# Tile starts at multiples of 256 bytes, and the low parts of the last stage's input chunks computed on GpSimd

## The chip, the cores and the metric

The kernel runs on one core of a Trainium2 chip. TensorE (PE in the profile; its weight loads are PEld), VectorE (DVE), ScalarE (ACT) and GpSimd (POOL) compute; SyncE (SP) issues the DMAs. The engines run side by side and wait for each other through semaphores. The metric is the device time of one execution in microseconds.

## The reference

For `x` of 2048 rows and 640 columns, the kernel computes `g * a + (1 - g) * b`, all in float32:

```python
g = sigmoid((x * gate_w).sum(-1, keepdims=True))
q, k, v = split(x @ wqkv, 32 heads of 20)
phi(p) = concat(softmax(p @ w_phi), softmax(-(p @ w_phi)))      # 40 features a head
kv, z = phi(k)^T v, phi(k).sum over the rows
a = ((phi(q) @ kv) / (phi(q) @ z + 1e-6)) @ wo
b = silu(x @ w1) @ w2                                            # 1728 hidden columns
```

`a` is linear attention: the keys and values of all rows are first summed into a small table per head (`kv`), then each row's query features are multiplied with it. `b` is a feed-forward block.

## The kernel before

To reach float32 accuracy on TensorE, every operand of a large product is held as a high part (the value rounded to TensorE's one-pass format) and a low part (the remainder). A product then takes three passes: high times high, high times low, low times high. The helper `split` (lines 120 to 123) makes the two parts: ScalarE copies the high part, and VectorE or GpSimd subtracts it from the source for the low part. Its two lines, 121 and 123, therefore carry the splits of all stages; tile names tell them apart.

The work runs in three stages, each ordered by hand (`inorder` fixes the order of instructions per engine; the DMA issues on SP are left to the framework's scheduler):

1. **Keys and values** (about 0 to 200 us of the span). The weights `wh`/`wl` (high and low part, two tiles of tag `big`) are formed, then 16 row tiles are projected (line 473, 500 and 282 columns at a time) and summed into `kv` (lines 443 and 454).
2. **Feed-forward** (about 200 to 560 us). For each of four blocks of 512 rows and each of 14 hidden tiles, `ph` (line 521) multiplies a tile of `w1` with `x`, and `acc` (line 709) multiplies a tile of `w2` with the activated hidden tile `u`. Each product streams 512 columns past a 128 by 128 weight tile; both have 15 matmuls for a hidden tile, 10 for the rest tile `w_r`.
3. **Queries and output** (about 560 to the end). Rows go in chunks of 256. A step (`step(u)`) transposes the features of chunk u (`pT`, line 990), projects two row tiles with the fused query weights (`pq`, line 432, 320 columns), multiplies features with `kv` (`pn`, line 1123), copies the numerators to `oT` (lines 1136 to 1146) and multiplies them with `wo` (`pa`, line 1165, 256 columns, 80 matmuls a chunk). VectorE takes maxima, differences and sums of the query features (lines 416 to 423, 794, 810); GpSimd multiplies the features with the normalizer and its inverse (lines 807 and 843) and adds the feed-forward part to the output (line 1183).

The input of stage 3, apart from the first chunks, comes through `raw` tiles: a chunk is three DMAs (`xb_load`, two of 512 columns' width and one of 256), and each is split by `xb_split` into an `xb` tile. `x_next(k)` splits the next k of them and issues the load of the one four further on into the `raw` tile that this frees (`x_ahead`). The line `xb_split(p, "dve")` puts the low part on VectorE. `step` calls `x_next(2)` at its start and `x_next(1)` in its middle. The first chunk's three splits are outside `x_next` and have the low part on GpSimd.

All tiles lie in pools that follow one another in SBUF. Each tile is rounded up to 32 bytes, so a tile's start follows from the sizes of all that stand before it:

| tiles | what they hold | start modulo 256, before |
|---|---|---|
| tag `big`, first | `wh`; later `f` tiles of hidden tiles 7, 8 and 9 (`w1`), 7 and 8 (`w2`); later `wo` | 128 |
| tag `big`, second | `wl`; later `f` tiles of hidden tiles 5, 6 (`w1`), 4, 5, 6 (`w2`); later `wq` | 0 |
| tag `raw`, four | inputs on arrival | 128, 160, 192, 224 |
| tags `x`, `w`, `u` | input chunks, weights of hidden tiles 0 to 4 (`w1`), 0 to 3 (`w2`), activations | 0 |
| pools `ta`, then `fp`, then `tb` | `ta`: features and values of stage 1; `fp`: `w1` of hidden tiles 10 to 12, `w2` of 9 to 12, `w_r`; `tb`: `oT`, the rest rows of `wo` (`wor_s`), `ez`, `y` | 224 |

In the feed-forward stage every weight slice (128 columns, 512 bytes) lies a multiple of 512 bytes behind its tile's start, so it has that tile's remainder.

Of the kernel before, what the change touches and what calls it, by code (L numbers as in the profile page):

```python
# [8 lines left out]
F32 = mybir.dt.float32  # L9
# [7 lines left out]
P = 128  # L17
S = 2048
D = 640
# [3 lines left out]
NC = D // P  # L23
# [7 lines left out]
GW = GR * DH  # L31
# [4 lines left out]
RC = 2 * REST  # L36
# [15 lines left out]
EB = 2  # L52
KXB = 1
WC = 2 * D + 2
WS = WC + 2
BIG = 2 * NC * D + 32
CUTS = (0, 500, 1000, WC)
RW = 114
NEARLY = 3
# [4 lines left out]
def mix_kernel(ctx: ExitStack, tc: tile.TileContext, xT, wqT, wkc, wkr, wv, bd, bdc, cst, wo, w1, w1r, w2, out):  # L64
    nc = tc.nc

    cp = ctx.enter_context(tc.tile_pool(name="cp", bufs=1))
    wp = ctx.enter_context(tc.tile_pool(name="wp", bufs=1))
# [3 lines left out]
    def opened(name, **kw):  # L72
        open_pools[name] = tc.tile_pool(name=name, bufs=1, **kw)
        return open_pools[name].__enter__()
# [6 lines left out]
    fu = opened("fu")  # L81
    ta = opened("ta")
# [16 lines left out]
        return ps.tile([P, 512], F32, tag=f"single{k % 4}", name=name, bufs=1)  # L99

    def raw(name):
        return wp.tile([P, D + 2], F32, tag="raw", name=name, bufs=4)

    def slot(name, pool=None, tag="x", bufs=7):
        return (pool or wp).tile([P, 2, 512], F32R, tag=tag, name=name, bufs=bufs)

    def big_tile(name):
        return wp.tile([P, BIG], F32R, tag="big", name=name, bufs=2)

    def big(name):  # L110
        return big_tile(name)[:, : 2 * NC * D].rearrange("p (c s d) -> p c s d", c=NC, s=2)
# [5 lines left out]
    def wslot(name, dt=F32):  # L117
        return fq.tile([P, 2 * D], dt, tag="w", name=name, bufs=NPRE)

    def split(hi, lo, src, lo_eng="dve"):  # L120
        nc.scalar.copy(hi, src)  # L121
        eng = nc.vector if lo_eng == "dve" else nc.gpsimd
        eng.tensor_tensor(lo, src, hi.bitcast(F32), op=ALU.subtract)  # L123
# [4 lines left out]
    @contextmanager  # L128
    def inorder(*engines):

        traced = nc.cur_bb.bb.instructions
        n = len(traced)
        yield
        prev = {}
        for i in traced[n:]:
            if i.engine in engines:
                if i.engine in prev:
                    tc.add_manual_dep(
                        i,
                        prev[i.engine],  # L140
                        mybir.DependencyInfo(mybir.DependencyClass.NoSync, mybir.DependencyReason.DATA),
                        reason="inorder",
                    )
                prev[i.engine] = i.name
# [6 lines left out]
    stk = cp.tile([P, 4], F32, name="stk")  # L151
    warms = cp.tile([P, 1], F32, name="warms")
    ones = cp.tile([P, P], F32R, name="ones")
    stage = [ta.tile([P, 2, 2 * D], F32, tag="ph", name=f"stage{k}", bufs=2) for k in range(2)]
    stf = [t.rearrange("p a d -> p (a d)") for t in stage]
    st0 = [t[:, k * D : (k + 1) * D] for t in stf for k in range(3)][:NC]
# [59 lines left out]
    def xb_split(p, lo_eng="pool"):  # L216
        u, c = XP[p]
        r = xb.pop(p)
        t = slot(f"xb_{u}_{c}")
        split(t[:, 0, : r.shape[1]], t[:, 1, : r.shape[1]], r, lo_eng)  # L220
        if c == 0:
            X["t", u] = []
        X["t", u].extend(t[:, :, k * 256 : (k + 1) * 256] for k in range(r.shape[1] // 256))
# [3 lines left out]
    def load_fused(gi):  # L227
        n = min(GW, D - gi * GW)
        rq[gi] = r = raw(f"wTq{gi}")[:, :D]
        nc.sync.dma_start(r[:n, :], wqT[gi * GW : gi * GW + n, :])  # L230
# [64 lines left out]
    def flat(name):  # L295
        return ta.tile([P, D + 2], F32, tag="kx", name=name, bufs=KXB)
# [45 lines left out]
    kvp1 = [None] + [ps.tile([P, 512], F32, name=f"kvq{k}") for k in (1, 2)]  # L342

    def v_weights(c):
        r = ta.tile([P, 2 * D], F32, tag="e", name="wvr1", bufs=EB)[:, : D + 2] if c == 1 else flat(f"wvr{c}") if c == 2 else raw(f"wvr{c}")
        nc.sync.dma_start(r, wv[c * P : (c + 1) * P, :])
        split(WKV[0][:, c, D:WC], WKV[1][:, c, D:WC], r)

# [367 lines left out]
    r = raw("w1rr")  # L716
# [4 lines left out]
    r = raw("w2rr")  # L721
# [9 lines left out]
    def wo_load(c):  # L731
        wor_raw[c] = r = raw(f"wo{c}")
        nc.sync.dma_start(r[:, :D], wo[c * P : (c + 1) * P, :])
# [146 lines left out]
    def kvl_load(k):  # L880
        kvb[k] = r = raw(f"kvl{k}")[:KD, :D]
        nc.sync.dma_start(r, kv_d[KD:KF, k * D : (k + 1) * D])

    def kvl_sum(k):

        r = kvb.pop(k)
        a = kvb["kvm"][:, k * D : (k + 1) * D]
        nc.vector.tensor_tensor(a, a, r, op=ALU.add)
# [53 lines left out]
    def load_gates(b):  # L942
        if b == 0:
            pg = bank("pg")
            nc.tensor.transpose(pg[:NT, :P], g1, ident)
            gT = fp.tile([NT, P], F32, name="gT")
            nc.scalar.copy(gT, pg[:NT, :P])
            nc.sync.dma_start(g_d, gT)
        gates[b] = fp.tile([P, 512], F32, tag="G1", name=f"G1_{b}", bufs=1)
        nc.sync.dma_start(gates[b], g_d.rearrange("t p -> (t p)")[b * 512 : (b + 1) * 512].partition_broadcast(P))  # L950
# [17 lines left out]
    def last_dense(n, *extra):  # L968

        part = h_parts(NB - 1, order[n])  # L970
        us[order[n]] = next(part)
        for w in extra:
            next(w)
        next(part)
        if 1 < n < NF:
            add(n - 2)
        for w in extra:
            next(w)
# [33 lines left out]
    with inorder(PE, DVE, ACT, POOL):  # L1012
        last_dense(2)
        last_dense(3)
        load_gates(NB - 1)
        load_fused(0)
        last_dense(4)
        WQ = big("wq")
        zbc = wslot("zbc")
        nc.sync.dma_start(zbc, kv_d[KF].partition_broadcast(P))  # L1020

        def fuse(gi):
            return fused(kvb["bd"], WQ[:, :, 0, :], WQ[:, :, 1, :], gi)

        load_fused(1)
        kvl_load(0)
        last_dense(5, fuse(0))
        kvl_sum(0)
        load_fused(2)
        kvl_load(1)  # L1030
        last_dense(6, fuse(1))
        kvl_sum(1)
        WO = big("wo")
        load_fused(3)
        wo_load(0)
        last_dense(7, fuse(2))
        wo_split(0)
        load_fused(4)
        wo_load(1)
        wo_load(2)  # L1040
        last_dense(8, fuse(3))
        wo_split(1)
        wo_split(2)
        load_fused(5)
        wo_load(3)
        wo_load(4)
        kvw = wslot("kvw")[:GW, : 2 * NG * CT].rearrange("p (j f) -> p j f", f=CT)
        kvwr = fu.tile([RC, GW], F32, name="kvwr")
        w = make_kvw()
        last_dense(9, w)  # L1050
        w = fuse(4)
        next(w)
        next(w)
        wo_split(3)
        wo_split(4)
        for p in range(3):
            xb_load(p)
        last_dense(10, fuse(5))
        t = 2 * NP - 4
        q_tile(t)  # L1060
        last_dense(11)
        q_rest(t)
        xb_split(0)
        t += 1
        q_tile(t)
        last_dense(12)
        q_rest(t)
        xb_split(1)
        t += 1
        q_tile(t)  # L1070
        last_dense(13)
        q_scale(t)
        t += 1
        q_open(t, q_proj(t))
        xb_split(2)
        acc_mm(0)
        q_feat(t)
        q_norm_sum(t - 1)
        q_parts(t - 1)
        acc_out(0)  # L1080
        q_inv(t - 1)
        q_weights(t - 1)
        q_mul(t - 1)
        q_norm(t)
        acc_mm(1)
        acc_out(1)
        acc_mm(2)
        acc_out(2)
        for i in range(4):
            t_mm(0, i, bank)  # L1090
            t_out(0, i)
        acc_mm(3)
        acc_out(3)
        q_sum(t)
        q_scale(t)
        acc_mm(4)
        acc_out(4)
        q_norm_sum(t)
        q_parts(t)
        q_inv(t)  # L1100
        q_weights(t)
        q_mul(t)
# [91 lines left out]

    def x_next(k):
        for p in range(xb_done[0], min(xb_done[0] + k, len(XP))):
            xb_split(p, "dve")
            x_ahead(p + 4)
            xb_done[0] = p + 1

# [21 lines left out]

    def step(u):
        a, b, c = 2 * u - 2, 2 * u - 1, 2 * u
        x_next(2)
        t_all(u, 0, 4)
        on(b, q_mm)
        on(a, q_norm_sum)
        t_all(u, 4, 6)
        spikes(b)  # L1230
        on(a, q_small)
        on(b, q_norm)
        on(a, q_mul)
        w_mm(u - 1, 0, 2)
        w_copy(u - 1, 0)
        w_add(u - 1, 0)
        on(b, q_sum)
        x_next(1)
        n_all(u)
        n_lo(u, 0)  # L1240
        on(b, q_norm_sum, q_small, q_mul)
        on(c, q_mm)
        w_mm(u - 1, 2, 2)
        spikes(c)
        w_copy(u - 1, 2)
        n_lo(u, 1)
        n_lo(u, 2)
        w_mm(u - 1, 4, 1)
        on(c, q_sum, q_norm)
        w_copy(u - 1, 4)  # L1250
        w_add(u - 1, 2)
        w_add(u - 1, 4)
# [109 lines left out]
```

## Time and profile before

| | |
|---|---|
| median of 3 runs | 756.83 us (756.64 to 757.03) |
| the profiled execution | 756.51 us, span 754.7 us from first to last instruction |
| TensorE busy | 748.6 us, 99% of the span, 4177 matmuls |
| VectorE, ScalarE, GpSimd busy | 370.0, 264.0, 243.9 us |
| granted TensorE clock | 1.00 throughout |

Views that are used below: the page's summary; the groups of instructions by line and tile (busy time, mean duration, idle time before them and who ended it); the chain of work that ended last, which gives start, length and number of instructions of each piece, so that length over number is the spacing from one matmul's start to the next; and the timeline, in which the columns are start, length, engine, line, operation and, in brackets, idle time of the engine and who ended it. A matmul's own duration (some 390 ns) overlaps with the next one's and isn't its price; the spacing is.

### The profile page before, as it was taken

How to read it: one execution, taken by the hardware profiler on the slowest of the kernel's cores; microseconds unless marked ns; L12 is line 12 of the kernel's file. 1: busy time of each engine (PE TensorE's matmuls, PEld its weight loads, DVE VectorE, ACT ScalarE, POOL GpSimd, SP SyncE). 2: the span in 40 equal slices, each digit the busy share in tenths (PEclk: the TensorE clock that was granted, in tenths of full speed). 3: DMA queues.
4: the chain of work that ended last, by engine and by line, in shares of the span. 5: the costliest groups of instructions: out<-in, count | busy, mean ns of one | idle time of the engine just before them, and what ended most of it. 6: DMA issues, size and time to landing. Idle time of an engine off the chain costs nothing.

```text
span 754.7 us, 10442 instructions
## 1 busy us (share of the span) xinstructions
PE 748.6 (99%) x4177; PEld 646.7 (86%) x4177; DVE 370.0 (49%) x634; ACT 264.0 (35%) x477; POOL 243.9 (32%) x143
## 2 busy tenths in 40 slices
PE   9999999999999999999999999999999999999998
PEld 7888888888888888888888888888898899999988
DVE  5676666676641221012210122123566898888752
ACT  5444444336542311113111121123453534345230
POOL 2488777768000000000000000000274367565540
PEclk9999999999999999999999999999999999999999
DMA  7111111113660120001200014122103132221222
GB/s 260 50 54 53 53 53 53 59 44 90 198 185 1 56 98 1 1 0 56 101 0 1 1 41 120 37 74 72 38 29 107 55 98 64 91 76 58 71 85 78
DMA packets 35304, 50.27 MB, mean 67 GB/s; under 512 B 3546, under 2 KB 22890, under 8 KB 35255
## 3 DMA queue, kind: packets, MB, share of 16 engines
q1 hardware_dynamic: 35255, 49.60, 20.9%
q8 instruction: 33, 0.54, 0.3%
q14 instruction: 16, 0.13, 0.1%
HBM read 38.48 MB, written 11.11 MB: 66 GB/s over the span
## 4 chain that ended last, share of the span: by engine, by line
PE 96%; DVE 2%; DMA 1%; issue 0%; ACT 0%; SPq 0%; DVEq 0%
PE acc L709 25%; PE ph L521 23%; PE kvp L473 16%; PE pa L1165 10%; PE pq L432 9%; PE pn L1123 3%; PE kv L443 2%; PE pT L990 2%; PE kvp L538 2%; PE kvp L331 1%; PE kvq L331 1%; PE pwq L234 1%; PE pwk L320 1%; DVE xb L123 1%; DMA wvr<-wv 1%
## 5 line engine op out<-in xcount | busy, mean ns | idle before, releaser
L123 DVE TENSOR_TENSOR u<-ph,u 128x512 fp32r<-128x512 f32 x48 | 33.2, 692 | 187.3 <-ACT u L121 187.3
L709 PE MATMUL acc<-u,w 128*128 128x512 f32 x480 | 115.2, 393 | 0.0
L709 PEld LDWEIGHTS acc<-u,w 128*128 128x128 f32 x480 | 89.6, 188 | 20.2
L892 POOL MEMSET kvw<- 120x40 f32 x1 | 0.1, 132 | 314.1 <-PE ph L521 314.1
L521 PE MATMUL ph<-xf,w 128*128 128x512 f32 x420 | 100.6, 392 | 0.0
L524 ACT ACTIVATE ph<-ph 128x512 f32<-128x512 f32 x48 | 27.9, 582 | 192.1 <-PE ph L521 192.0
L521 PEld LDWEIGHTS ph<-xf,w 128*128 128x128 f32 x420 | 78.7, 188 | 17.5
L473 PE MATMUL kvp<-wh,xa 128*128 128x500 f32 (+1 forms) x420 | 93.0, 357 | 0.0
L473 PEld LDWEIGHTS kvp<-wh,xa 128*128 128x128 f32 x420 | 71.4, 189 | 10.0
L1165 PE MATMUL pa<-oT,wo 128*128 128x256 f32 x600 | 77.8, 283 | 0.0
L807 POOL TENSOR_TENSOR ez<-eq,zbc 128x1280 f32<-128x1280 f32 x16 | 47.0, 2935 | 92.7 <-ACT eq L790 55.1
L1165 PEld LDWEIGHTS pa<-oT,wo 128*128 128x128 f32 x600 | 74.6, 189 | 0.8 <-DVE oT L1144 0.8
L709 PE MATMUL acc<-u,f 128*128 128x512 f32 x300 | 72.3, 392 | 0.0
L521 PE MATMUL ph<-xf,f 128*128 128x512 f32 x300 | 72.3, 392 | 0.0
L521 PEld LDWEIGHTS ph<-xf,f 128*128 128x128 f32 x300 | 56.4, 188 | 12.5
L709 PEld LDWEIGHTS acc<-u,f 128*128 128x128 f32 x300 | 56.2, 188 | 12.2
L432 PE MATMUL pq<-wq,xb 128*128 128x320 f32 x360 | 56.3, 313 | 1.0 <-DVE xb L123 0.8
L123 POOL TENSOR_TENSOR ph<-ek,ph 128x1280 fp32r<-128x1280 f32 x16 | 47.5, 2969 | 27.4 <-ACT ph L121 27.4
L432 PEld LDWEIGHTS pq<-wq,xb 128*128 128x128 f32 x360 | 52.9, 188 | 3.5 <-issue 1.6
L473 PE MATMUL kvp<-wl,xa 128*128 128x500 f32 (+1 forms) x210 | 47.6, 357 | 0.0
L790 ACT ACTIVATE eq<-eq 128x1280 f32<-128x1280 f32 x16 | 20.4, 1275 | 67.9 <-DVE eq L423 67.9
L501 POOL TENSOR_TENSOR ek<-ek,st 128x1280 f32<-128x1280 f32 x16 | 37.9, 2369 | 9.1 <-issue 6.1
(159 smaller groups left out, 1070.0 us busy)
## 6 DMA issues: line engine op xcount, KB each, us to landing
wr<-w SPq DMA_DIRECT2D x26, 320.0 KB, 3.9
xrf<-xT SPq DMA_DIRECT2D x20, 256.0 KB, 3.7
fb_d<-o SPq DMA_DIRECT2D x20, 256.0 KB, 2.4
y<-fb_d SPq DMA_DIRECT2D x16, 256.0 KB, 3.0
out<-y SPq DMA_DIRECT2D x16, 256.0 KB, 2.1
xra<-xT SPq DMA_DIRECT2D x14, 256.0 KB, 3.0
xrb<-xT SPq DMA_DIRECT2D x12, 256.0 KB, 2.6
wvr<-wv SPq DMA_DIRECT2D x5, 321.0 KB, 5.2
```

The costliest lines, as they stand in the source:

```text
L123: eng.tensor_tensor(lo, src, hi.bitcast(F32), op=ALU.subtract)
L331: nc.tensor.matmul(kv_cols(t, lo, hi), x_of(t)[c][:, hx, :], WKV[hw][:, c, lo:hi], start=(opens and hx == 0 and hw == 0), stop=(c == NC - ...
L432: nc.tensor.matmul(dst, xt[c][:, hx, :], w[:, c, hw, lo : lo + n], start=first, stop=(hx == 1 and c == NC - 1))
L473: nc.tensor.matmul(kv_cols(t, lo, hi), xt[c][:, hx, :], WKV[hw][:, c, lo:hi], start=(n == 0), stop=(n == 3 * NC - 1), skip_group_check=True,)
L501: nc.gpsimd.tensor_tensor(groups(e), groups(e), spread(st[:, 1, :]), op=ALU.mult)
L521: nc.tensor.matmul(ph, lhs, rhs, start=(n == 0), stop=(n == len(todo) - 1))
L524: nc.scalar.activation(hs, ph, AF.Silu)
L709: nc.tensor.matmul(acc[m], lhs, rhs, start=(f == order[0] and n == 0), stop=(f == order[-1] and n == len(todo) - 1))
L790: nc.scalar.activation(Q[t]["e"], Q[t]["e"], AF.Exp)
L807: nc.gpsimd.tensor_tensor(ez, Q[t]["e"], zbc, op=ALU.mult)
L1123: nc.tensor.matmul(pns[u, gp][side * CT : side * CT + lhs.shape[-1], a, :], lhs, f[:w, k * 256 : (k + 1) * 256], start=True, stop=True,)
L1165: nc.tensor.matmul(pa[:, a, :], WO[:, c, hw, ds] if c < NG else WOR[:, ds], o[:, ho, c, :] if c < NG else o[:GW, ho, c, :], start=(k == 0) ...
```

## The change

Four sizes change, one unused tile of 128 bytes is added, and the splits in `x_next` change their engine and place:

```diff
-BIG = 2 * NC * D + 32
+RAW = D + 16
+BIG = 2 * NC * D + 64
...
     def raw(name):
-        return wp.tile([P, D + 2], F32, tag="raw", name=name, bufs=4)
+        return wp.tile([P, RAW], F32, tag="raw", name=name, bufs=4)
...
     ones = cp.tile([P, P], F32R, name="ones")
+    cp.tile([P, 32], F32, name="pad")
...
-        r = ... else raw(f"wvr{c}")
+        r = ... else raw(f"wvr{c}")[:, : D + 2]
...
-        kvwr = fu.tile([RC, GW], F32, name="kvwr")
+        kvwr = fu.tile([RC, P], F32, name="kvwr")[:, :GW]
...
     def x_next(k):
         for p in range(xb_done[0], min(xb_done[0] + k, len(XP))):
-            xb_split(p, "dve")
+            xb_split(p)
...
     def step(u):
         a, b, c = 2 * u - 2, 2 * u - 1, 2 * u
-        x_next(2)
+        x_next(3)
...
         on(b, q_sum)
-        x_next(1)
         n_all(u)
```

Counted through: the constants' pool begins at byte 16,512 and had 1,280 bytes, so the first `big` tile began at 17,792 (69 times 256, and 128); with the pad it begins at 17,920 (70 times 256). A `big` tile grows from 25,728 to 25,856 bytes (101 times 256). The four `raw` tiles grow from 2,592 to 2,624 bytes each, 10,496 together (41 times 256); one by one they begin at remainders 0, 64, 128 and 192. `kvwr` grows from 480 to 512 bytes. The pools `ta`, `fp` and `tb` then begin at 175,360 (685 times 256) in place of 174,816 (682 times 256, and 224). So the `f` tiles, `wo`, the weights in `fp`, `oT` and `wor_s` all begin at multiples of 256 bytes. The rows of `wh` and `wl` are 5,136 bytes apart before and after, so their slices still begin at many remainders.

`xb_split(p)` without an engine puts the low part on GpSimd, in that engine's order at the place of the call: three low parts at the start of each of the steps 1 to 5 (15 instructions), ahead of the step's other work on GpSimd. The high parts stay on ScalarE; the third of each step moves from the middle to the start of ScalarE's order. The third load of a step is issued right after the two others.

More of the change, by code (lines that the diff above doesn't have):

```diff
@@ L344, in v_weights @@
     def v_weights(c):
-        r = ta.tile([P, 2 * D], F32, tag="e", name="wvr1", bufs=EB)[:, : D + 2] if c == 1 else flat(f"wvr{c}") if c == 2 else raw(f"wvr{c}")
+        r = ta.tile([P, 2 * D], F32, tag="e", name="wvr1", bufs=EB)[:, : D + 2] if c == 1 else flat(f"wvr{c}") if c == 2 else raw(f"wvr{c}")[:, : D + 2]
         nc.sync.dma_start(r, wv[c * P : (c + 1) * P, :])
```

## The prediction, made before the result was known

> **What bounds the kernel now.** First the page's head and its chain: TensorE is busy 99% of the span and carries 96% of the chain that ended last. Only two things can make this kernel faster: matmuls that follow each other more closely, or fewer waits of TensorE.
>
> ```profile
> span 754.7 us, 10442 instructions
> PE 748.6 (99%) x4177; PEld 646.7 (86%) x4177; DVE 370.0 (49%) x634; ACT 264.0 (35%) x477; POOL 243.9 (32%) x143
> ...
> PE 96%; DVE 2%; DMA 1%; issue 0%; ACT 0%; SPq 0%; DVEq 0%
> ```
>
> Next the chain of waits inside the feed-forward stage (second block of rows). Columns: start, length, piece, number of matmuls; nothing waits between the pieces.
>
> ```profile
> 299.65 3.40 PE acc L709 x15
> 303.05 3.40 PE ph L521 x15
> 306.45 3.41 PE acc L709 x15
> 309.86 3.49 PE ph L521 x15
> ...
> 325.98 3.48 PE acc L709 x15
> 329.46 3.49 PE ph L521 x15
> 332.95 3.49 PE acc L709 x15
> 336.44 3.50 PE ph L521 x15
> ...
> 345.77 3.50 PE acc L709 x15
> ```
>
> These are matmuls of one shape, yet they come at different spacings. By the order of the hidden tiles and the table of starts, the first three (`w2` of tile 3, `w1` of 6, `w2` of 4) have weights at remainder 0: 10.21 / 45 = 226.9 ns. 309.86 (`w1` of 7), 329.46 (`w1` of 9) and 325.98, 332.95 (`w2` of 7 and 8) have remainder 128: 13.95 / 60 = 232.5 ns. 336.44 (`w1` of 10) and 345.77 (`w2` of 9) have 224: 233.3 ns. Low addresses are slow (first `big` tile), middle ones fast, the highest slow again, so it is the remainder that fits, not the place.
>
> The last stage I read by the timeline, a steady step (from 647) beside the first one (from 598); each from the first `pn` over 24 `pn`, 30 `pq` and 48 `pa` matmuls to the next transposes.
>
> ```profile
> 598.28 2.38 PE L1123 MATMUL pn<-fT,kvw 120*64 120x256 f32 x20
> ...
> 601.33 2.49 PE L432 MATMUL pq<-wq,xb 128*128 128x320 f32 x14 [0.23 <-DVE sm L837]
> 604.62 2.61 PE L432 MATMUL pq<-wq,xb 128*128 128x320 f32 x16 [0.80 <-DVE xb L123]
> ...
> 612.81 1.37 PE L990 MATMUL pT<-ident,eq 128*120 128x128 f32 x11
> ```
>
> ```profile
> 647.23 2.38 PE L1123 MATMUL pn<-fT,kvw 120*64 120x256 f32 x20
> ...
> 660.21 1.91 PE L990 MATMUL pT<-ident,eq 128*120 128x128 f32 x16
> ```
>
> The same work takes 12.98 us in a steady step and 14.53 us in the first, so the two waits cost 1.55 us with the restarts behind them. The bracket names the low part `xb` on VectorE as one cause and a small VectorE instruction queued behind another `xb` as the other.
>
> **The change part by part.**
>
> *512-column matmuls.* The groups give the numbers.
>
> ```profile
> L709 PE MATMUL acc<-u,w 128*128 128x512 f32 x480 | 115.2, 393 | 0.0
> L521 PE MATMUL ph<-xf,w 128*128 128x512 f32 x420 | 100.6, 392 | 0.0
> ...
> L709 PE MATMUL acc<-u,f 128*128 128x512 f32 x300 | 72.3, 392 | 0.0
> L521 PE MATMUL ph<-xf,f 128*128 128x512 f32 x300 | 72.3, 392 | 0.0
> ...
> L709 PE MATMUL acc<-u,w_r 128*128 128x512 f32 x40 | 10.0, 395 | 0.0
> ```
>
> Of the 300 `ph<-xf,f`, three of five tiles lie in the first `big` tile (180 matmuls); of the 300 `acc<-u,f`, two of five (120): 300 at remainder 128. Of the 420 `ph<-xf,w`, 180 lie in `fp` (3 tiles, 15 matmuls, 4 blocks); of the 480 `acc<-u,w`, 240; with 40 of `w_r` in `acc` and 40 in `ph`, 500 at remainder 224. All come to 226.9 ns. The gain is 300 x 5.6 = 1.7 us and 500 x 6.4 = 3.2 us, 4.9 together. Ends: 0, if the start isn't the cause, and 800 x 6.4 = 5.1. Nothing covers or eats this gain: in these rows TensorE follows itself.
>
> A rule speaks against it. The Trainium skill, page "TensorE: Matmul & The Clock Gate", section "Step-by-step: what each phase is for", says that weights come through a read port of their own, so that loading the next ones takes no read bandwidth from the running matmul. By that alone a weight tile's start shouldn't change the spacing, and this term would be 0. The rows above differ by weights alone, so here the trace doesn't agree with it.
>
> *256-column matmuls of the output.* Both operands (`oT` at 224, `wo` at 128) become aligned, and no aligned row of that shape exists. The nearest rows by shape, from the chain in the key stage and in the last one:
>
> ```profile
> 102.17 6.82 PE kvp L473 x30
> ...
> 109.33 1.95 PE kvp L473 x15
> ```
>
> ```profile
> 614.73 4.40 PE pq L432 x30
> ...
> 654.64 5.73 PE pa L1165 x48
> ```
>
> Unaligned: 282 columns 130.0 ns, 500 columns 227.3, 512 columns about 233, and `pa` itself, 256 columns, 119.4. These lie near one line, about 0.445 ns a column and 5 ns. Aligned: `pq`, 320 columns, 146.7 ns, and 512 columns, 226.9: 0.418 ns a column and 13.0 ns. The lines cross near 280 columns; at 256 the aligned one gives 120.0 ns. So I take 640 x (120.0 - 119.4) = 0.4 us lost. The gaining end is a saving as large as that of a 512-column matmul, 6 ns: 640 x 6.0 = 3.8 us. I take the line, since it meets two aligned shapes and the other meets four unaligned ones.
>
> *Keys and values.* `wh` moves by 128 bytes, but its rows are 5,136 bytes apart, so slices keep beginning at all sorts of remainders, as they do in both halves now (227.3 and 130.0 above). I take 0. The ends are 0.5 us either way, about 1 ns on 420 + 70 matmuls.
>
> *The first loads.* Input and weight rows land at other remainders, and TensorE waits once for what they feed:
>
> ```profile
> 8.82 0.56 PE L331 MATMUL kvp<-wh,xa 128*128 128x360 f32 x2 [0.41 <-ACT wh L121]
> ```
>
> Bounds are a gain or a loss of that wait, 0.4 us; I take 0, since the transfer also reads memory, whose rows don't change. The Trainium skill, page "DMA: Bandwidth & Descriptors", section "How a descriptor splits into AXI transactions", has an unaligned transfer start with a partly unused 256-byte piece: a row of 2,568 bytes from remainder 224 would be 88 beats in place of 81, an estimate from that page. By it the wait would vanish.
>
> *Low parts to GpSimd.* Prices by the groups and the tile's own list:
>
> ```profile
> L123 DVE TENSOR_TENSOR xb<-xrb,xb 128x512 fp32r<-128x512 f32 x10 | 14.9, 1523 | 2.8 <-ACT xb L121 2.8
> ...
> L123 DVE TENSOR_TENSOR xb<-xrb,xb 128x256 fp32r<-128x256 f32 x5 | 9.2, 1849 | 0.0
> ```
>
> ```profile
> L123 POOL TENSOR_TENSOR xb<-xrb,xb x3: 733/1290/1294, 549.5 to 567.0; 128x512 fp32r<-128x512 f32 x2, 128x256 fp32r<-128x256 f32 x1
> ```
>
> VectorE loses 14.9 + 9.2 = 24.1 us, 4.8 a step; GpSimd gets 2 x 1.29 + 0.73 = 3.3 us a step. GpSimd's own steps, and what it does in one step:
>
> ```profile
> 591.54 2.94 POOL L807 TENSOR_TENSOR ez<-eq,zbc 128x1280 f32<-128x1280 f32 x1 [5.40 <-ACT eq L790]
> ...
> 652.66 1.30 POOL L1183 TENSOR_TENSOR y<-pac,y 128x512 f32<-128x512 f32 x1
> 654.07 2.37 POOL L843 TENSOR_TENSOR eq<-eq,sm 128x1280 f32<-128x1280 f32 x1
> 659.08 2.93 POOL L807 TENSOR_TENSOR ez<-eq,zbc 128x1280 f32<-128x1280 f32 x1 [2.64 <-ACT eq L790]
> 661.96 2.90 POOL L1183 TENSOR_TENSOR y<-pac,y 128x512 f32<-128x512 f32 x2
> 670.95 2.91 POOL L807 TENSOR_TENSOR ez<-eq,zbc 128x1280 f32<-128x1280 f32 x1 [6.09 <-DVE sm L837]
> ```
>
> ```profile
> 636.68:660.37 23.69, 23.69 (x189) 22.43 (x187) 20.80 (x30) 10.05 (x18) 14.84 (x8) 1.00 0.26 84
> ```
>
> The three pieces stand between 664.86 and 670.95, where GpSimd idles 6.09 us: they end at about 668.2, 2.8 us ahead of the next product, at no cost. Without that cover they would delay the feature product (654.07 to 656.44), which the transposes at 660.21 need: 3.8 us more of slack. In step 1 GpSimd ends its `ez` at 594.5 and the pieces at 597.8, before `pq` reads them (from 601). VectorE, rid of two `xb` there, waits for that `ez` instead and comes about 1 us sooner to line 837, for which TensorE waited 0.23 us. Both waits go: 1.55 us gained. Ends: 0 (VectorE still late) and 1.55.
>
> ScalarE's third copy comes ahead of the copies of the transposes; it delays these by 0.4 us, and TensorE reuses their banks only after 4.4 us of `pq`. SP: the three loads now wait for GpSimd's pieces; behind them in SP's queue may stand the output stores and the loads of `y`. These can come some 3.5 us later, and the addition that needs `y` (652.66 in the steady step, so 676.3 in the next) is after two more GpSimd products. I take 0; its price if it fails is rival D.
>
> *Sum*, against the profiled execution (756.51 us): - 4.9 + 0.4 - 1.55 = - 6.05, that is 750.5 us. The median shown is 0.3 us higher than that execution.
>
> **The rivals.**
> A: the 256-column matmuls gain like the 512-column ones. For it: same engine, both operands moved. Against: the two lines. 750.5 - 0.4 - 3.8 = 746.3 us.
> B: the start isn't the cause, and the alignment does nothing: only the 1.55 us remain, 755.0 us. Against it stand all nine feed-forward rows. (The skill's rule on weight loads, above, would have it so.)
> C: the alignment gains, but the first step's waits stay, because another VectorE or ScalarE instruction is as late: 752.0 us.
> D, the slower side: GpSimd's pieces, and behind them the loads and stores on SP, make the feature product late in every step. It takes a delay beyond the 3.8 us of slack; for a loss over all, TensorE must lose over 6.05 + 1.5 us in five steps, 1.5 a step, so a delay over 5.3 us. If pieces of 3.3 us behaved as three times as long (6.6 more, 2.8 beyond the slack), five steps would lose 14 us: 756.5 - 4.5 + 14 = 766 us. Against: by the window above (busy time of PE, PEld, DVE, ACT and POOL) GpSimd is 14.84 of 23.69 us busy in a step.
>
> **How the numbers follow.** Main case 0.55, A 0.27, C 0.08, B 0.06, D 0.04. About 0.2%, 1.5 us, is what can be told from no change. Main, A and C are faster; B lies just at that bound, and I count two thirds of it as same. Range 745.8 to 752.3: from A to C with half a microsecond for the first loads and the key stage; it leaves out B and D. The main case alone: 749.6 to 751.4.
>
> **What would show it.** All feed-forward pieces of 15 at 3.40 us; one that keeps 3.49 or 3.50 falsifies the first term. `pa` pieces of 48 at 5.76 us (main) or 5.45 (A). The first step's 14.53 us become 12.98, with no bracket naming `xb`, and steady steps stay at 23.7 us. Wrong would be a TensorE wait on GpSimd at the transposes (D), or a new wait of `pq` on ScalarE's copies (C).

## The result, and the profile after

The changed kernel takes 749.68 us (749.52 to 750.11) against 756.77 us: ratio 0.9907, 95% interval 0.989 to 0.9924. The forecast was 750.5 us, in a range of 745.8 to 752.3. The profiled execution took 749.73 us with a span of 748.0 us, 6.8 us less than the one before; the sum had said 6.05.

In the changed file most lines stand two further down (`ph` is line 523, `acc` 711, `pq` 434, `pa` 1167), the low part of `split` one further, at 124. The page's head and chain after:

```profile
span 748.0 us, 10444 instructions
PE 742.9 (99%) x4177; PEld 647.2 (87%) x4177; DVE 347.6 (46%) x619; ACT 263.8 (35%) x477; POOL 255.2 (34%) x158
...
PE 98%; DMA 1%; SPq 0%; ACT 0%; DVE 0%; issue 0%
```

TensorE has the same 4177 matmuls and is as full as before; VectorE, 2% of the chain before, has all but left it. The chain inside the same block of the feed-forward stage, with the same hidden tiles as in the prediction:

```profile
301.36 3.40 PE ph L523 x15
304.76 3.40 PE acc L711 x15
308.16 3.40 PE ph L523 x15
...
324.02 3.40 PE acc L711 x15
327.43 3.40 PE ph L523 x15
330.82 3.40 PE acc L711 x15
334.23 3.40 PE ph L523 x15
...
343.29 3.40 PE acc L711 x15
```

Every piece of 15 is at 3.40 us: the spacing is now 226.7 ns whichever pool holds the weights. The pieces that were at 3.48 to 3.50 are those from 308.16 on, except the `acc` pieces of tiles 5 and 6. In the key stage the chain shows a small shift that the prediction had left at 0: matmuls of 500 columns follow each other a little closer, those of 282 columns a little further apart:

```profile
102.14 6.77 PE kvp L475 x30
...
109.24 1.97 PE kvp L475 x15
```

The first step of the last stage, by TensorE's timeline:

```profile
592.85 2.38 PE L1125 MATMUL pn<-fT,kvw 120*64 120x256 f32 x20
...
595.59 4.66 PE L434 MATMUL pq<-wq,xb 128*128 128x320 f32 x30
...
605.85 1.91 PE L992 MATMUL pT<-ident,eq 128*120 128x128 f32 x16
```

`pq` is one piece of 30 without a bracket. From the first `pn` to the transposes it is 13.00 us, where it was 14.53. Of the last stage's pieces, those of 48 output matmuls got longer by the chain, 5.76 us in place of 5.73; those of 32 stayed at 3.82:

```profile
600.25 5.76 PE pa L1167 x48
```

Added over the spacings from one matmul's start to the next: the 800 feed-forward matmuls with formerly unaligned weights gave 4.8 us and the aligned ones beside them 0.3; `pq` and `pn` gave 1.6; the key stage 0.5; `pa` took 0.2, and the first 25 us took 0.1.

### The profile page after: what moved, and what is told of

Same layout as the page of the kernel before. It is cut to its first block, busy times and chain, and to the rows that moved or that the text cites. A ratio compares the mean times of both kernels' runs of the same rounds, so it can differ in the third digit from the quotient of the medians.

```text
span 748.0 us, 10444 instructions
## 1 busy us (share of the span) xinstructions
PE 742.9 (99%) x4177; PEld 647.2 (87%) x4177; DVE 347.6 (46%) x619; ACT 263.8 (35%) x477; POOL 255.2 (34%) x158
## 4 chain that ended last, share of the span: by engine, by line
PE 98%; DMA 1%; SPq 0%; ACT 0%; DVE 0%; issue 0%
PE acc L711 25%; PE ph L523 23%; PE kvp L475 16%; PE pa L1167 10%; PE pq L434 10%; PE pn L1125 3%; PE pT L992 2%; PE kv L445 2%; PE kvp L540 2%; PE kvp L333 1%; PE kvq L333 1%; PE pwq L236 1%; PE pwk L322 1%; DMA wvr<-wv 1%; PE kvp L456 0%; SPq L187 0%
## 5 line engine op out<-in xcount | busy, mean ns | idle before, releaser
L711 PE MATMUL acc<-u,w 128*128 128x512 f32 x480 | 113.6, 390 | 0.0
```

Of the source, the lines that this page charges most:

```text
L711: nc.tensor.matmul(acc[m], lhs, rhs, start=(f == order[0] and n == 0), stop=(f == order[-1] and n == len(todo) - 1))
```

## The experiments

The two theories to be told apart: the gain consists of two independent parts, operand starts (about 4.5 us) and the low parts' move (1.55 us); or one of them does all. Then, for the starts: an unaligned start lengthens the time per column, so that 512-column matmuls lose and 256-column ones do not (two lines); or it costs a fixed amount per matmul; or only weights count.

**The sizes alone** (`align_only`):

```diff
-            xb_split(p)
+            xb_split(p, "dve")
...
-        x_next(3)
+        x_next(2)
...
+        x_next(1)
         n_all(u)
```

> The changed kernel's sizes, but the low parts of the xb tiles on VectorE and at their old two places. Theory (two separate gains): feed-forward pieces of 15 matmuls at 3.40 us, output pieces of 48 at 5.76 us, and in the first step the stretch from pn to the next transposes back at 14.5 us with waits on the xb low part; about 1.55 us slower than the changed kernel, 751.2 us. Rival (the new starts of the raw tiles are what made the low parts come in time): VectorE's xb of 512 columns falls clearly below 1523 ns, the first step stays near 13.0 us, and the time is that of the changed kernel, 749.7 us.

Measured: 751.16 us (750.78 to 751.53), ratio 0.9926 (0.9912 to 0.994). TensorE's timeline in the first step has its two waits back:

```profile
592.63 2.38 PE L1125 MATMUL pn<-fT,kvw 120*64 120x256 f32 x20
...
595.69 2.49 PE L434 MATMUL pq<-wq,xb 128*128 128x320 f32 x14 [0.25 <-DVE sm L839]
598.98 2.61 PE L434 MATMUL pq<-wq,xb 128*128 128x320 f32 x16 [0.80 <-DVE xb L124]
...
607.19 1.04 PE L992 MATMUL pT<-ident,eq 128*120 128x128 f32 x8
```

That is 14.56 us, and the group of `xb` stays at 1518 ns. So the starts of the `raw` tiles have nothing to do with it.

**The move alone** (`move_only`):

```diff
-            xb_split(p, "dve")
+            xb_split(p)
...
-        x_next(2)
+        x_next(3)
...
-        x_next(1)
```

> The old sizes, with the low parts of the xb tiles on GpSimd at the start of each step. Theory: the first step falls from 14.53 to about 13.0 us, nothing else moves; 756.8 - 1.55 = 755.2 us. Rival (the waits go only because TensorE's spacing changed): the first step stays above 14 us and the time at 756.8 us.

Measured: 755.34 us (754.83 to 755.77), ratio 0.998 (0.9971 to 0.9989). The first step's stretch runs from 598.23 to 611.21, 12.98 us. The two parts add up: 756.83 - 751.16 = 5.7 and 756.83 - 755.34 = 1.5, together 7.2, against 7.1 for the whole change.

**The engine without the place** (`engine_only`): the changed kernel with the third split back in the middle of the step.

```diff
-        x_next(3)
+        x_next(2)
...
+        x_next(1)
         n_all(u)
```

> The changed kernel, but the third split of a step stays in the middle of the step; its low part then stands in GpSimd's order behind the addition to the output. Theory (the place is as necessary as the engine): that addition ends some 4.0 us after pq begins (653.96 against 649.97 in the steady step of the kernel before), the low part 0.7 us later, and pq reads it after about 2.0 us, so TensorE waits about 2.7 us in each of five steps: about 13 us slower than the changed kernel, 763 us. Rival (the engine alone matters): no wait, 749.7 us.

Measured: 770.0 us in a single execution, 20 us slower than the changed kernel and 13 slower than the kernel before. From 590 us on, by the view of waits, TensorE waits for nothing but the low part, five times, 12.9 us in all, of which 4.2 us in the first step and 2.2 in each of the others:

```profile
PE pq L434 <- POOL xb L124: 12.9, 5, 4.2
```

The chain of one step, in order of time:

```profile
639.96 4.42 PE pq L434 x30
...
644.40 0.82 DVE mmq L418
...
651.67 2.38 POOL eq L845
654.05 0.69 POOL y L1185
...
655.22 0.74 POOL xb L124
655.96 0.04 issue
656.00 4.15 PE pq L434 x16
...
667.65 4.42 PE pq L434 x30
```

The mechanism of the wait is the expected one, and so is its size, since 13 us were expected. The chain shows why the low part is late again in each step: the late `pq` makes the maxima late, these the exponentials and GpSimd's products, and behind those stands the next low part for which `pq` waits.

What wasn't expected is the rest of the loss. The 16 `pq` matmuls behind the wait take 4.15 us above, but 2.61 us one step earlier, behind a wait of the same length:

```profile
629.85 2.61 PE L434 MATMUL pq<-wq,xb 128*128 128x320 f32 x16 [2.17 <-POOL xb L124]
```

The granted TensorE clock is 0.59 from 656.00 to 660.15 us and 1.00 from 629.80 to 632.50. Over four of the five pieces behind a wait it is 0.59 to 0.62, and these take 3.93 to 4.15 us, about 5.8 us more together than at the full clock. So a step with the lower clock takes 27.7 us (639.96 to 667.65), 4.0 us more than the steady 23.7, and the step ahead of it 26.15 us (613.81 to 639.96), 2.4 us more. Waits and clock are 18.7 of the 20 us; the rest isn't assigned, and why the clock fell behind four of the waits and not behind the fifth stays open.

**The place without the engine** (`place_only`): three splits at the start, low parts on VectorE.

```diff
-            xb_split(p)
+            xb_split(p, "dve")
```

> The changed kernel with all three splits at the start of a step, but their low parts on VectorE. Theory (VectorE's load early in the step is what counts): VectorE spends 4.8 us at the start of a step in place of 2.9, so the wait for line 837's successor in the first step grows from 0.2 to about 2 us while the wait for the third low part goes; the first step's stretch comes to about 15.3 us, the steady steps stay at 23.7 us, and the time is about 752.0 us. Rival (only the late third split mattered): the first step at about 13.3 us, 750.0 us.

Measured: 750.28 us in a single execution, nearer to the rival. The stretch is 13.61 us, with one wait left:

```profile
592.79 2.38 PE L1125 MATMUL pn<-fT,kvw 120*64 120x256 f32 x20
...
596.14 4.67 PE L434 MATMUL pq<-wq,xb 128*128 128x320 f32 x30 [0.53 <-DVE sm L839]
...
606.40 1.80 PE L992 MATMUL pT<-ident,eq 128*120 128x128 f32 x15
```

The expectation took the three pieces at their old prices, 4.8 us. Their groups say why it was wrong:

```profile
L124 DVE TENSOR_TENSOR xb<-xrb,xb 128x512 fp32r<-128x512 f32 x10 | 15.1, 1552 | 2.7 <-ACT xb L122 2.7
...
L124 DVE TENSOR_TENSOR xb<-xrb,xb 128x256 fp32r<-128x256 f32 x5 | 4.3, 850 | 0.0
```

The 256-column piece took 1849 ns in the middle of the step, beside GpSimd's product of 2.9 us, and takes 850 ns at the start, where the third piece mostly finds GpSimd free. So of the 1.56 us, taken in this order, 0.95 (14.56 to 13.61) come from the earlier place and 0.6 from the other engine.

**The streamed operand unaligned** (`x_at_128`): the tiles of tag `x` at remainder 128. The weights of `ph` and both operands of `acc` stay aligned; the starts of the `raw` tiles and of some `fT` tiles move too. (In this kernel lines stand one further down, in the next one some stand one further up.)

```diff
-RAW = D + 16
+RAW = D + 8
...
         load_x("a", 1)
+    wp.tile([P, 32], F32, name="pad2")
```

> The changed kernel with only the x tiles (input chunks) moved to remainder 128: they are streamed in ph and are the weights in pq and in the key stage. Theory (two lines: a matmul with either operand unaligned takes about 5 ns + 0.445 ns a column, an aligned one 13 ns + 0.417 ns): ph goes from 226.7 to about 232.5 ns (820 matmuls with those of line 540, 4.8 us), pq of 320 columns only from 146.7 to about 147.4 ns (0.3 us), acc stays at 226.7; about 754.8 us. Rival (only the weights' start counts, at a fixed price of 6 ns a matmul): ph stays at 226.7 ns, pq goes to about 152.7 ns (480 matmuls, 2.9 us); about 752.6 us.

Measured: 756.1 us (755.66 to 756.23), nearly all of the gain gone with aligned weights. The chain:

```profile
310.87 3.49 PE ph L524 x15
314.36 3.43 PE acc L712 x15
```

```profile
614.23 4.40 PE pq L435 x30
```

`ph`, whose streamed `x` is unaligned, is at 3.49 us, as it was with unaligned weights; `pq` of 320 columns, whose weights these tiles are, stays at 4.40. That fits the two lines and not the fixed price. What wasn't expected is `acc`: both of its operands are aligned, and it takes 3.43 us between unaligned `ph` pieces (about 0.9 us in all). Added over the spacings, another 0.3 us went in the key stage, whose weights these tiles are, and 0.2 in the first 25 us.

**The weights unaligned** (`big_at_128`): both `big` tiles at remainder 128 (`wh`, `wl` and `wq` with them), `oT` and `fp` aligned.

```diff
-RAW = D + 16
+RAW = D + 24
...
-    cp.tile([P, 32], F32, name="pad")
```

> The changed kernel with only the two big tiles moved to remainder 128: the f tiles and wo are weights, wq is streamed. oT stays aligned. Theory (two lines): the 600 feed-forward matmuls on f tiles take 232.5 ns (3.5 us more), pa of 256 columns goes down from 120.0 to about 119.4 ns (0.4 us less), pq from 146.7 to 147.4 ns (0.3 us more); about 753.1 us. Rival (fixed price of 6 ns for an unaligned weight tile, whatever the number of columns): pa goes up to about 126 ns (3.6 us more), pq stays; about 756.8 us.

Measured: 753.61 us (753.29 to 754.02). By the chain, feed-forward pieces on the `f` tiles are at 3.48 to 3.49 us, and the output, whose weights `wo` are unaligned, is a little faster than with all aligned (5.76), as the two lines have it; the fixed price would have made it 6.05:

```profile
329.49 3.48 PE ph L522 x15
332.97 3.49 PE acc L710 x15
```

```profile
604.39 5.72 PE pa L1166 x48
```

In the key stage, which streams `wh` and `wl`, the pieces are back at the values of the kernel before:

```profile
102.37 6.82 PE kvp L474 x30
...
109.51 1.94 PE kvp L474 x15
```

**The last pools at 64** (`fp_at_64`):

```diff
-        kvwr = fu.tile([RC, P], F32, name="kvwr")[:, :GW]
+        kvwr = fu.tile([RC, P + 16], F32, name="kvwr")[:, :GW]
```

> The changed kernel with the pools fp, ta and tb moved to remainder 64: weights of the last hidden tiles, and oT, which pa streams; wo stays aligned. Theory (two lines; only multiples of 256 are aligned): the 500 feed-forward matmuls on fp tiles take about 233 ns (3.2 us more), pa goes from 120.0 to about 119.4 ns (0.4 us less); about 752.5 us. Rival 1 (64 bytes are enough): all stays, 749.7 us. Rival 2 (fixed price for any unaligned operand): pa about 126 ns, 756.5 us.

Measured: 751.86 us in a single execution. The feed-forward pieces on `fp` weights are at 3.50 us, so a multiple of 64 bytes isn't enough. But `pa` fell further than the line has it (5.73):

```profile
341.23 3.50 PE ph L523 x15
344.73 3.50 PE acc L711 x15
```

```profile
603.79 5.60 PE pa L1167 x48
```

**The output's operands one by one.** Four kernels move `oT` and `wo` alone among TensorE's operands; `ez`, `y` and the copies of `pa`, which lie behind `oT` in its pool, move with it. `ot_at_64` and `ot_at_128` lengthen `wor_s`, which stands before `oT`, by 16 or 32 numbers, and the others also move `wo` inside its `big` tile by 32 or 16:

```diff
-    WOR = tb.tile([GW, D], F32R, name="wor_s")
+    WOR = tb.tile([GW, D + 16], F32R, name="wor_s")[:, :D]
...
-        WO = big("wo")
+        WO = big_tile("wo")[:, 32 : 32 + 2 * NC * D].rearrange("p (c s d) -> p c s d", c=NC, s=2)
```

> The changed kernel with wor_s longer by 64 bytes, so that oT, which pa streams, begins at remainder 64; all weights stay aligned. Theory (an unaligned streamed operand shortens a matmul of 256 columns, as the run with the pools at 64 showed): pa falls from 120.0 to about 117.3 ns, 640 matmuls, 1.5 to 1.7 us less than the changed kernel, 748.1 us. Rival (that gain came from another tile of the shifted pools, such as ez or y): pa stays at 120.0 ns and the time at 749.7 us.

> The same with oT at remainder 128. If any unaligned start does the same, pa takes about 117.3 ns and the time is 748.1 us; if the two lines hold with one price for the unaligned, 119.4 ns and 749.3 us; if the remainder itself counts, another value.

> oT at remainder 64 and wo at remainder 128 (moved inside its tile; the f tiles stay aligned). Theory A (the two starts act on their own): pa is at the 117.3 ns of oT alone less the 1 ns that wo alone gave, 116.3 ns, 747.6 us. Theory B (the weights' start decides once it is unaligned): about 119.2 ns as with wo alone, 749.2 us.

> oT at remainder 64 and wo at remainder 128 once more, with enough executions for an interval. If its single execution of 746.9 us holds: pa pieces of 48 at 5.49 us, 746.9 us, a ratio of about 0.987 to the kernel before and 2.8 us below the changed kernel. If it was chance: nearer to 748.5 us, the time with oT alone moved.

> oT and wo both at remainder 64. If the two starts act on their own and any unaligned weight start does the same: 114.4 ns as with wo at 128, 746.9 us. If it counts that the two remainders differ: pa near the 117.3 ns of oT alone or above, 748.3 us or more.

Measured, with the starts modulo 256, each row from the chain's pieces of 48 `pa`:

| kernel | `oT` start | `wo` start | piece of 48, us | one, ns | time, us |
|---|---|---|---|---|---|
| before | 224 | 128 | 5.73 | 119.4 | 756.8 |
| after | 0 | 0 | 5.76 | 120.0 | 749.68 |
| `big_at_128` | 0 | 128 | 5.72 | 119.2 | (other weights moved too) |
| `ot_at_128` | 128 | 0 | 5.70 to 5.71 | 118.9 | 749.1, one execution |
| `ot_at_64` | 64 | 0 | 5.60 | 116.7 | 748.48 (748.25 to 749.07) |
| `ot_64_wo_64` | 64 | 64 | 5.72 | 119.2 | 749.7, one execution |
| `ot_64_wo_128`, `best` | 64 | 128 | 5.49 | 114.4 | 746.9 once, then 746.75 (746.73 to 746.83) |

The expected gain of `ot_at_64` came (116.7 ns, 117.3 were expected), with the same 5.60 us as in `fp_at_64`; `ot_at_128` has another value, so the remainder itself counts. That it is `oT`, and not `ez` or `y`, no run shows by itself, since these move with it; it is argued from the trace: TensorE doesn't read them and waits for nothing in these steps, and GpSimd's `ez` takes 2931 ns beside 2936 in the changed kernel. `wo` is isolated by the last three rows: beside `oT` at 64, it gives 5.60, 5.72 and 5.49 us at 0, 64 and 128. So the two starts don't act on their own, and neither theory for `ot_64_wo_128` (116.3 or 119.2 ns) holds: `wo` at 128 helps beside `oT` at 64 more than beside `oT` at 0, and `wo` at 64 takes the gain back. A difference of 0.02 us between two rows needn't come from these starts: `x_at_128`, with both at 0, has pieces of 5.74 us where the changed kernel has 5.76. The last kernel, run again as `best`, has the ratio 0.9866 to the kernel before (0.985 to 0.9883) and is 2.9 us faster than the changed kernel:

```profile
600.13 5.49 PE pa L1167 x48
```

## Why the prediction was right, step by step

- **512-column matmuls, 4.9 us.** Measured 4.8 us on the 800 matmuls concerned, now at 226.7 ns by the chain shown. `align_only`, which has all the new starts and not the move, gives 5.7 us of the 7.1. The row reading (remainder, not place) held: `big_at_128` and `fp_at_64` bring 3.48 to 3.50 back exactly where they unalign the weights.
- **Rival B** is out: a weight tile's start alone moves the spacing from 226.7 to 232.5 ns (`big_at_128`), as the streamed operand's start does (`x_at_128`). The Trainium skill, page "TensorE: Matmul & The Clock Gate", section "Step-by-step: what each phase is for", says that loading the next weights takes no read bandwidth from the running matmul. By that alone this term would have been 0; the measurement decides.
- **256-column matmuls, 0.4 us lost.** Measured 0.2 us: the piece of 48 came out at 5.76 us, the value that the aligned line gave, but the pieces of 32 stayed at 3.82. The part of the step that failed is the other line: one price for the unaligned isn't so at 256 columns. It depends on both remainders, from 114.4 to 119.4 ns, and the line met only the pair that the kernel before happened to have. So it was partly luck that the loss was small: measured from the pair of `best`, aligned starts lose 5.6 ns a matmul. (The two lines, with the coefficients given, cross near 296 columns, not 280; the value at 256 doesn't change by it.) Rival A is out for the aligned start, but its time (746.3) was nearly reached by `best`, by another way.
- **The first step's waits, 1.55 us.** Measured 14.53 to 13.00 us; `move_only` gives 1.5 us by itself. GpSimd had the room, by its timeline in a steady step after:

```profile
655.01 2.00 POOL L1185 TENSOR_TENSOR y<-pac,y 128x512 f32<-128x512 f32 x2
656.96 3.25 POOL L124 TENSOR_TENSOR xb<-xrb,xb 128x512 fp32r<-128x512 f32 x3
```

  The pieces take 3.25 us, 3.3 were assumed, and they start earlier than assumed, since the two additions ahead of them fell from 2.90 to 2.00 us. Before, these ran beside VectorE's `xb`; with the low parts back on VectorE at the start of the step (`place_only`) they take as long as before. The group of these additions in the kernel before, in the changed one and in `place_only`:

```profile
L1183 POOL TENSOR_TENSOR y<-pac,y 128x512 f32<-128x512 f32 x10 | 14.8, 1476 | 0.0
```

```profile
L1185 POOL TENSOR_TENSOR y<-pac,y 128x512 f32<-128x512 f32 x10 | 13.0, 1299 | 0.0
```

```profile
L1185 POOL TENSOR_TENSOR y<-pac,y 128x512 f32<-128x512 f32 x10 | 14.8, 1482 | 0.0
```

  The Trainium skill, page "SBUF — State Buffer", section "Who interferes with whom", says that a VectorE instruction with two inputs in SBUF contends with a GpSimd one that reads SBUF. The trace agrees, for both engines: 1476 to 1299 ns for GpSimd's addition, 1849 to 850 ns for VectorE's third piece when it was moved apart (`place_only`).
- **Rival D** didn't come up: in SP's timeline the stores go ahead of the loads that wait for GpSimd, and no TensorE wait names GpSimd. `engine_only` shows that a loss through GpSimd was possible, at another place than D had it: with one low part behind one addition, it isn't the transposes that wait but `pq`, and the kernel loses 20 us, 12.9 of them in waits.
- **Keys and values, taken as 0, with 0.5 us as the end.** It was the end, a gain of 0.5 us: 500 columns from 6.82 to 6.77 us for 30, 282 columns from 1.95 to 1.97 for 15. That slices keep beginning at many remainders was no reason for 0: with `wh` and `wl` at 128 (`big_at_128`) both values go back. This is most of the 0.7 us by which the sum fell short; the other terms came out near their sizes, each where it was expected.
- **The first loads, taken as 0.** The wait stayed, 0.41 us before and 0.44 after in the timeline's bracket, at 8.97 in place of 8.82. The loads of these rows did land a little sooner, by the pages before and after (the last number is the median from issue to landing, in us):

```profile
wvr<-wv SPq DMA_DIRECT2D x5, 321.0 KB, 5.2
```

```profile
wvr<-wv SPq DMA_DIRECT2D x5, 321.0 KB, 5.0
```

  That is about 4%. The estimate from the Trainium skill, page "DMA: Bandwidth & Descriptors", section "How a descriptor splits into AXI transactions", 81 beats in place of 88 for a row from remainder 224, would be 8%, and the wait would have vanished by it.
- **The range.** Its upper end, from C with half a microsecond, would be 752.5 and not 752.3; this decides nothing here.

## What to carry to other kernels

Where TensorE is full, compare the spacing of matmuls of one shape across operands: two spacings for one shape mean that something about the operands, here their start modulo 256 bytes, has a price that no wait shows. Align both operands of 512-column matmuls; for 256 columns measure, since there the aligned start was among the slowest. When work moves to another engine, its place in that engine's order counts as much as the engine, and a wait that this brings into a full TensorE can cost more than its length.

## What was not expected of the hardware

- With 256 columns, two unaligned operands can be faster than two aligned ones: 114.4 ns at remainders 64 and 128, 119.2 at 64 and 64, 120.0 at 0 and 0 (119.6 in `x_at_128`). Which property of the pair decides stays open; seven pairs were run, and none with a remainder between 0 and 64.
- Behind waits of 2.2 to 4.2 us (`engine_only`) the granted TensorE clock was 0.59 to 0.62 over the next 16 matmuls in four of five cases, which then took 3.93 to 4.15 us in place of 2.61.
- Aligned `acc` matmuls between unaligned `ph` ones take 3.43 us for 15, and 3.40 between aligned ones.
- Unaligned streamed and unaligned weight tiles cost a 512-column matmul about the same (3.49 us each for 15), and a 320-column matmul nothing that can be seen (4.40 us for 30 either way).
